# A chunked attention and a SoLU layer: the first eight tiles in a written order, weights converted 1024 columns at a time

## The chip, the cores and the metric

The program runs on one core of a Trainium2 chip. The metric is the device time of one execution in microseconds (us). Five engines run their own instruction streams and wait for each other by semaphores: TensorE (PE in the profile; its weight loads PEld), VectorE (DVE), ScalarE (ACT), GpSimd (POOL) and SyncE (SP), which here only issues transfers.

## The reference

```python
def _attn_ref(q, k, v):                 # 8 batches, 8 heads, 576 positions, 64 wide
    scores = scale * np.matmul(q_c, k_c.transpose(0, 1, 2, 4, 3))   # inside chunks of 64
    scores = scores - np.max(scores, axis=-1, keepdims=True)
    attn = np.exp(scores)
    attn = attn / (np.sum(attn, axis=-1, keepdims=True) + 1e-09)
    out = np.matmul(attn, v_c)

def _moe_ref(x, w_in, w_out, g_ln):     # x: 4608 x 512, from the attention's output
    h = x @ w_in                        # 512 x 1024
    sm = softmax(h)                     # written out with max, exp, sum + 1e-9
    solu = h * sm
    mu, var = mean(solu), mean((solu - mu) ** 2)
    ln = (solu - mu) / np.sqrt(var + 1e-06) * g_ln
    return (ln @ w_out).astype(np.float32)     # 1024 x 512
```

w_in and w_out arrive as 64-bit floats; the kernel reads them as pairs of 32-bit words.

## The kernel before, in words

The 4608 rows are 36 tiles of 128 rows (two chunks of 64). A tile passes these steps: q and k are turned so that their 64 columns lie on partitions (qT, kT); `scores` (16 small products into the PSUM tile sx); `softmax_a` (maximum and difference on VectorE, exponential on ScalarE), `softmax_b` (sum, reciprocal, division); the attention is turned (attn_t); `values` (16 small products, sx again); the result is split into a high and a low part (x_h, x_l); `ffn_in`, 24 products of 512 columns into ph; `solu_a` (maximum h_nmax, exponential) and `solu_b` (the product with h, then the mean); `variance`; z is turned and split (z_h, z_l); `ffn_out` in three thirds of 8 products (po), each started by `third`; `store`. Products with weights use three terms, high by low, high by high and low by high, with the types float32r for both parts. The names are those of the profile.

The weights are converted once from 64-bit words to a high part (wi_h for w_in, wo_h for w_out times g_ln) and a low part (wi_l, wo_l). Before the change this goes in 16 pieces of 512 columns. `piece_scale` takes the absolute value of the upper word, scaled (ScalarE, w_a). `piece_top` clamps it to a range (VectorE or POOL), shifts it left by 3 (VectorE), puts the sign back (VectorE, SCALAR_TENSOR_TENSOR w_a<-w_raw,w_a), masks the exponent (w_p), forms the lower word's part w_r from that (POOL or VectorE), and rounds the high part (ScalarE). `piece_rest` makes the low part: for the ten pieces in `D_PE` by three products on TensorE (the value by the identity or by a diagonal of g_ln, a plain float32 product; minus the high part; w_r) and an evacuation, for three by two such products after a subtraction elsewhere, for three without TensorE.

Tiles 0 to 4 come from a table of words, START, that names the steps in turn (`C:1` converts the next piece, `M:2` is `ffn_in(2)`, `F` a third of an output product). Their order on each engine is set by the library's scheduler from a model of durations, since `order.on` is false there: only from tile 5 on do instructions keep the program's order. From tile 5 a loop runs over the tiles; in an iteration i it does `ffn_in(i)`, the scores of tiles 8, 9 and so on ahead, and the output product of tile i - 3. Tiles 0 to 4 take q and k by natural loads (nat, two halves, one for even and one for odd tiles) and turn them on TensorE (`N`); from tile 5 on they come from loads of a batch in blocks of 32 columns (q_st, k_st), which VectorE turns (`qk_turn`). The raw words w_raw of unit 1 share a buffer with nat's tag z_t, those of units 2 to 7 alternate in the buffers of q_st and k_st, two of each.

Of the kernel before, what the change touches and what calls it, by code (L numbers as in the profile page):

```python
# [8 lines left out]
F32 = mybir.dt.float32  # L9
# [9 lines left out]
P0 n:0 P1 N:0 P:1 n:1 S:0 C:1 P:2 A:0 B:0 P:3 g C:1 n:2 N:1 C:1 C:1 v:0 T:0 C:1 P:4 C:1  # L19
S:1 N:2 C:1 n:3 C:1 C:1 A:1 P:5 P:6 v:1 B:1 V:0 S:2 T:1 M:0 X:0 C:1 A:2 v:2 C:1 P:7 N:3  # L20
B:2 Y:0 C:1 V:1 Q:1 T:2 C:1 n:4 S:3 A:3 v:3 q:8 R:0 V:2 M:1 q:8 X:1 N:4 B:3 S:4 C:1 A:4
q:8 Y:1 M:2 z:0:0 q:8 K:5 X:2 Y:2 T:3 V:3 K:6 C:1 z:0:1 R:1 Q:2 S:5 B:4 T:4 A:5 S:6 v:4
V:4 B:5 T:5 v:5 F F A:6 K:7 C:1 B:6 C:1 R:2 M:3 v:6 Z:2 F z:1:0 X:3 Y:3 S:7 K:8 M:4 q:14 R:3
z:1:1 X:4 A:7 B:7 Y:4 V:5 U:6 F U:7 q:18 Z:3 R:4 v:7 F F
# [3 lines left out]
class Order:  # L28
# [5 lines left out]
    def engine(self, engine):  # L34
        order = self

        class Ordered:
            def __getattr__(self, name):
                make = getattr(engine, name)

                def call(*args, **kwargs):
                    ins = make(*args, **kwargs)  # L42
# [8 lines left out]
def chunk_attention_then_solu_ffn(  # L51
# [90 lines left out]
    pieces = [("in", m, n) for m in range(NCC) for n in range(2)]  # L142
    pieces += [("out", m, 0) for m in range(NFC)]
    def load_pair(x):
# [12 lines left out]
        if x == 0:  # L157
            for n in range(2):
                cols = slice(n * HALF * raw_words, (n + 1) * HALF * raw_words)
                early[n:n] = [(dst[:, cols], src[:, cols])]  # L160
        else:
            nc.sync.dma_start(dst, src)
        for half in range(2):
            raws[pieces[2 * x + half]] = raw[:, half]

    scaled, tops = {}, {}

    def piece_scale(x):

        hi = raws[pieces[x]][:, :, 1]
        y = scaled[x] = work.tile(
            [P, HALF], F32, name="w_a", tag=("w_a", "o_sb")[x % 2]
        )
        act.activation(y, hi.bitcast(F32), AF.Abs, scale=2.0 ** -112)

    def piece_top(x):

        kind, m, n = pieces[x]
        raw = raws.pop(pieces[x])
        lo, hi = raw[:, :, 0], raw[:, :, 1]
        a = scaled.pop(x)
        (pool if x in MIN_POOL else dve).tensor_scalar(
            out=a, in0=a, scalar1=1.875 * 2.0 ** -96, scalar2=0.0, op0=ALU.min, op1=ALU.max
        )
        r = work.tile([P, HALF], F32R, name="w_r")
        if x in R_ACT:  # L190
            act.activation(r, lo, AF.Copy, scale=2.0 ** -52)
        elif x not in R_DVE:
            pool.tensor_scalar(
                out=r, in0=lo, scalar1=2.0 ** -52, scalar2=0.0, op0=ALU.mult, op1=ALU.add
            )
# [21 lines left out]
        if kind == "in":
            cols = slice(n * HALF, (n + 1) * HALF)
            top, d = wi_h[:, m, cols], wi_l[:, m, cols]
            act.copy(top, a)  # L220
            if x not in D_PE:
                (pool if x in D_POOL else dve).tensor_tensor(
                    out=d, in0=a, in1=top.bitcast(F32), op=ALU.subtract
                )
        else:
            top, d, g = wo_h[:, m, :], wo_l[:, m, :], g_sb[:, m:m + 1]
            act.activation(top, a, AF.Copy, scale=g)
            if x not in D_PE:
                dve.scalar_tensor_tensor(
                    out=d, in0=a, scalar=g, in1=top.bitcast(F32),  # L230
                    op0=ALU.mult, op1=ALU.subtract,
                )
        tops[x] = a, top, d, r

    def piece_rest(x):

        kind, m, n = pieces[x]
        a, top, d, r = tops.pop(x)
        if x in LO_TT and x not in D_PE:
            if kind == "in":  # L240
                (pool if x in LO_POOL else dve).tensor_tensor(
                    out=d, in0=d.bitcast(F32), in1=r.bitcast(F32), op=ALU.add
                )
            else:
                dve.scalar_tensor_tensor(
                    out=d, in0=r.bitcast(F32), scalar=g_sb[:, m:m + 1],
                    in1=d.bitcast(F32), op0=ALU.mult, op1=ALU.add,
                )
            return
        if kind == "in":  # L250
            one, one_r = ident, ident_r
        else:
            one_r = small.tile([P, P], F32R, name="g_diag_r", bufs=2)
            one = small.tile([P, P], F32, name="g_diag", bufs=2)
            for t in (one, one_r) if x in D_PE else (one_r,):
                (dve if x in G_DVE else pool).tensor_scalar(
                    out=t, in0=ident, scalar1=g_sb[:, m:m + 1], scalar2=0.0,
                    op0=ALU.mult, op1=ALU.add,
                )
        ps = ps_o.tile([P, HALF], F32, name="po")  # L260
        if x in D_PE:
            pe.matmul(ps, one, a, start=True, stop=False)
            pe.matmul(ps, minus_r, top, start=False, stop=False)
        else:
            pe.matmul(ps, ident_r, d, start=True, stop=False)
        pe.matmul(ps, one_r, r, start=False, stop=True)
        if x in LO_DVE:
# [579 lines left out]
```

## Time and profile before

| | |
|---|---|
| median of 3 runs | 511.1 us (510.99 to 511.14) |
| the profiled execution | 511.61 us, span 509.8 us |
| busy over the span: TensorE, VectorE, ScalarE, POOL | 478.0, 396.1, 265.0, 179.0 us |
| mean granted TensorE clock | 0.983 |
| chain of waits that ended last | TensorE 79%, VectorE 10% |

The profile has a row for each instruction or group: start, duration, engine, line of the kernel, operation, what it writes and reads, count, and in square brackets the idle time before it and what released it. Most instructions come from the helper in line 42 (49 after the change), so names of tiles tell more than lines. A table of stretches gives the busy time of each engine between two moments, with the granted clock of TensorE (1.00 is full), the share of the transfer engines and their rate. In the groups' rows the numbers behind the bar are busy us, mean ns of one, and idle time before. A plain float32 product of 512 columns and a small product show as two rows or a double count each.

### The profile page before, as it was taken

What the parts mean: (1) busy time and instruction counts of PE and PEld (TensorE: products, weight loads), DVE (VectorE), ACT (ScalarE), POOL (GpSimd) and SP (SyncE); (2) the same over time, 40 slices, a digit from 0 to 9 for tenths busy, and PEclk for the clock granted to TensorE, in tenths of its full rate; (3) what the DMA queues carried; (4) which work ended last, traced back from release to release, by engine and by line L of the source; (5) the groups of instructions that cost most, each with busy time, mean ns of one, the idle gap of its engine ahead of it and who ended that gap; (6) DMA issues with size and microseconds to landing.
All of it is one profiled execution on the core that took longest, in us unless ns stands there. A gap on an engine that the chain in (4) does not pass through costs nothing.

```text
span 509.8 us, 11183 instructions
## 1 busy us (share of the span) xinstructions
PE 478.0 (94%) x4190; PEld 385.7 (76%) x4190; DVE 396.1 (78%) x570; ACT 265.0 (52%) x448; POOL 179.0 (35%) x329
## 2 busy tenths in 40 slices
PE   3676969999999999999999999999999999999996
PEld 2354646777888888888888888888888888888875
DVE  5998967797886988797978887879788887854421
ACT  4755963644545545354555546455454453534442
POOL 4583961262514143232415050504151423323300
PEclk9987979999999999999999999999999999999999
DMA  9997799262878677868744859676761716153211
GB/s 278 346 230 138 126 149 133 40 149 59 189 125 200 128 188 155 195 121 181 155 118 111 165 148 160 162 144 176 137 165 47 187 39 186 46 141 97 69 43 41
DMA packets 204454, 72.33 MB, mean 142 GB/s; under 512 B 188592, under 2 KB 189104, under 8 KB 204016
## 3 DMA queue, kind: packets, MB, share of 16 engines
q1 hardware_dynamic: 197552, 58.23, 52.9%
q0 software_dynamic: 6272, 12.60, 9.5%
q8 instruction: 33, 0.54, 0.5%
q10 hardware_dynamic: 576, 0.79, 0.4%
q14 instruction: 21, 0.17, 0.1%
HBM read 36.97 MB, written 9.44 MB: 91 GB/s over the span
## 4 chain that ended last, share of the span: by engine, by line
PE 79%; DVE 10%; SPq 3%; ACT 3%; DMA 2%; issue 2%; POOL 0%; ACTq 0%; DVEq 0%
PE po L42 37%; PE ph L42 35%; DVE w_a L42 4%; PE sx L42 4%; PE tp L42 4%; SPq L42 3%; DMA w_raw<-in_moe_w_in_dram 1%; ACT z L42 1%; DVE h_nmax L42 1%; DVE w_p L42 1%; DVE z L42 1%; DVE s_sum L42 1%; DVE s_e L42 1%; DMA attn_t<-a_b 1%; DMA k_st<-in_k_dram 0%
## 5 line engine op out<-in xcount | busy, mean ns | idle before, releaser
L42 PE MATMUL ph<-wi_l,x_h 128*128 128x512 f32 x288 | 114.6, 398 | 5.5 <-ACT x_h L42 4.8
L42 PE MATMUL ph<-wi_h,x_h 128*128 128x512 f32 x288 | 114.1, 396 | 0.0
L42 PE MATMUL po<-wo_l,z_h 128*128 128x512 f32 (+1 forms) x288 | 113.6, 394 | 0.3 <-ACT z_h L42 0.2
L42 PE MATMUL po<-wo_h,z_l 128*128 128x512 f32 (+1 forms) x288 | 111.7, 388 | 0.0
L42 ACT ACTIVATE z<-ph,h_nmax 128x1024 f32<-128x1024 f32 x36 | 40.2, 1117 | 137.3 <-DVE h_nmax L42 137.3
L42 PE MATMUL po<-wo_h,z_h 128*128 128x512 f32 (+1 forms) x288 | 111.5, 387 | 0.0
L42 POOL TENSOR_TENSOR u<-ssq,eps 128x1 f32<-128x1 f32 x36 | 7.3, 203 | 218.6 <-ACT sq L42 218.6
L42 PE MATMUL ph<-wi_h,x_l 128*128 128x512 f32 x288 | 79.5, 394 | 0.0
L42 POOL DMA_DIRECT2D z_t<-z_b x136 | 67.9, 506 | 17.7 <-DVE z_b L42 12.3
L42 DVE TENSOR_REDUCE h_nmax<-ph 128x1 f32<-128x1024 f32 x36 | 44.0, 1222 | 35.2 <-PE ph L42 35.2
L42 PEld LDWEIGHTS ph<-wi_l,x_h 128*128 128x128 f32 x288 | 55.1, 191 | 19.3 <-ACT x_h L42 6.9
L42 PEld LDWEIGHTS ph<-wi_h,x_h 128*128 128x128 f32 x288 | 55.1, 191 | 11.4
L42 PEld LDWEIGHTS ph<-wi_h,x_l 128*128 128x128 f32 x288 | 54.5, 190 | 11.8 <-DVE x_l L42 0.3
L42 PEld LDWEIGHTS po<-wo_l,z_h 128*128 128x128 f32 x288 | 54.1, 188 | 12.2 <-ACT z_h L42 0.9
L42 PEld LDWEIGHTS po<-wo_h,z_l 128*128 128x128 f32 x288 | 54.1, 188 | 11.5 <-DVE z_l L42 0.4
L42 PEld LDWEIGHTS po<-wo_h,z_h 128*128 128x128 f32 x288 | 54.1, 188 | 10.4
L42 DVE TENSOR_TENSOR z_l<-z_t,z_h 128x1024 fp32r<-128x1024 f32 (+1 forms) x35 | 40.7, 1163 | 20.9 <-ACT z_h L42 20.9
L42 DVE SCALAR_TENSOR_TENSOR z<-ph,z 128x1024 f32<-128x1024 f32 x36 | 44.0, 1221 | 14.5 <-ACT z L42 14.5
L42 ACT ACTIVATE z<-z,z_sum 128x1024 f32<-128x1024 f32 x31 | 35.8, 1154 | 22.1 <-DVE z L42 21.6
L42 DVE STREAM_TRANSPOSE z_b<-z 128x1024 f32<-128x1024 f32 x33 | 39.9, 1208 | 3.2 <-ACT z L42 3.1
L42 ACT ACTIVATE o_sb<-po,r 128x512 f32<-128x512 f32 (+1 forms) x36 | 24.3, 676 | 30.1 <-POOL r L42 21.2
L42 ACT ACTIVATE sq<-z 128x1024 bf16<-128x1024 f32 x36 | 37.6, 1045 | 2.2 <-POOL z L42 2.2
(105 smaller groups left out, 687.9 us busy)
## 6 DMA issues: line engine op xcount, KB each, us to landing
out_dram<-o_sb SPq DMA_DIRECT2D x33, 256.0 KB, 2.5
v_sb<-in_v_dram SPq DMA_DIRECT2D x32, 256.0 KB, 4.2
z_t<-z_b POOLq DMA_DIRECT2D x128, 64.0 KB, 2.6
z_t<-z_b SPq DMA_DIRECT2D x128, 64.0 KB, 2.9
q_st<-in_q_dram SPq DMA_DIRECT2D x112, 72.0 KB, 3.3
k_st<-in_k_dram SPq DMA_DIRECT2D x112, 72.0 KB, 2.9
w_raw<-in_moe_w_out_dram SPq DMA_DIRECT2D x4, 1024.0 KB, 8.6
attn_t<-a_b SPq DMA_DIRECT2D x60, 64.0 KB, 3.7
```

What stands on the lines that cost most here:

```text
L42: ins = make(*args, **kwargs)
```

## The change

- All engines, SP too, keep the order in which the program names the instructions, in the start as well. START is written anew, with steps cut at their hand-overs from one engine to another: each function with a `yield` is entered once for each time that its word stands in the table, and does the next part.
- The conversion goes by 8 units of 1024 columns. POOL (VectorE for unit 4) clamps the upper word with its sign to a symmetric range; ScalarE applies a parametric ReLU whose negative slope is -2^32; VectorE shifts by 3, which brings that factor's exponent bit to the sign's place, so the step for the sign is gone. VectorE masks and forms w_r, always. All 16 halves make their low part by three products on TensorE; ScalarE evacuates 14 of them, VectorE two. POOL builds two diagonals of g_ln for each half of w_out.
- q and k of tiles 5 to 9 are loaded naturally and turned on TensorE; seven of the 20 copies out of PSUM go to VectorE. Batch 1 is not loaded in blocks any more.
- In the start, the softmax's division goes from POOL to VectorE; the mean of tile 3 goes from POOL to ScalarE. The loop is as before except that its first iteration doesn't turn tile 9, and the blocks of a batch are loaded up to those that a turn needs.

```diff
@@ the table START: two lines of each
-P0 n:0 P1 N:0 P:1 n:1 S:0 C:1 P:2 A:0 B:0 P:3 g C:1 n:2 N:1 C:1 C:1 v:0 T:0 C:1 P:4 C:1
-S:1 N:2 C:1 n:3 C:1 C:1 A:1 P:5 P:6 v:1 B:1 V:0 S:2 T:1 M:0 X:0 C:1 A:2 v:2 C:1 P:7 N:3
...
+P0 n:0 v:0 P1 P:1 n:1 P:2 v:1 P:3 N:0:0 N:0:1 N:0:0 n:2 N:0:1 g P:4 S:0 c:0 A:0 c:0 A:0 C:0 B:0
+c:1 t:0 c:1 r:0 T:0 T:0 N:1:0 C:1 N:1:1 D:0:1 N:1:0 t:1 r:1 D:0:0 D:0:1 V:0 N:1:1 D:0:0 c:2
...
@@ the helper through which every engine is called
-                    return order.tc.keep_in_program_order(ins) if order.on else ins
+                    return order.tc.keep_in_program_order(ins)
...
+    EV_DVE = ((1, 0), (5, 1),)
+    NV_DVE = ((0, 0), (0, 1), (1, 0), (1, 1), (3, 0), (6, 0), (9, 1),)
+    MEAN_POOL = (0, 1, 2, 4,)
+    CL_POOL = (0, 1, 2, 3, 5, 6, 7,)
...
+    def unit_scale(x):
+        hi = raws[x][:, :, :, 1]
+        y = scaled[x] = work.tile([P, 2, HALF], F32, name="w_a")
+        top = 1.875 * 2.0 ** 16
+        (pool if x in CL_POOL else dve).tensor_scalar(
+            out=y, in0=hi.bitcast(F32), scalar1=top, scalar2=-top, op0=ALU.min, op1=ALU.max
+        )
+        yield
+        act.activation(y, y, AF.Prelu, scale=2.0 ** -112, alpha=-(2.0 ** 32))
...
+        dve.tensor_scalar(
+            out=au, in0=au, scalar1=3, scalar2=None, op0=ALU.logical_shift_left
+        )
...
+    def unit_high(x):
+        if kind == "in":
+            act.copy(top, a)
+        else:
+            for y in range(2):
+                act.activation(top[:, y], a[:, y], AF.Copy, scale=g)
...
+    def unit_low(x):
+        dve.tensor_scalar(
+            out=ru, in0=au, scalar1=0xFF800000, scalar2=None, op0=ALU.bitwise_and
+        )
+        dve.scalar_tensor_tensor(
+            out=r, in0=lo, scalar=2.0 ** -52, in1=ru.bitcast(F32),
+            op0=ALU.mult, op1=ALU.mult,
+        )
...
+    def unit_rest(x, y):
+        ps = ps_o.tile([P, HALF], F32, name="po")
+        pe.matmul(ps, one, a[:, y], start=True, stop=False)
+        pe.matmul(ps, minus_r, top[:, y], start=False, stop=False)
+        pe.matmul(ps, one_r, r[:, y], start=False, stop=True)
+        yield
+        if (x, y) in EV_DVE:
+            dve.tensor_copy(out=d, in_=ps)
+        else:
+            act.copy(d, ps)
...
-        (dve if order.on else pool).tensor_tensor(
+        dve.tensor_tensor(
             out=e, in0=e, in1=rinv.unsqueeze(2).to_broadcast([P, H, CH]), op=ALU.mult,
...
@@ the word loop
+        if word in begun:
+            next(begun[word], None)
+            continue
+        step = todo[name](*map(int, arg))
+        if step is not None:
+            begun[word] = step
+            next(step, None)
...
@@ the loop from tile 5
             z_turn(i - 1)
-            turn(i + 4)
+            load_batch(next_batch)
+            next_batch += 1
```

VectorE, from its first row of the conversion on. Before, each piece of 512 columns has the clamp and shift (two TENSOR_SCALAR w_a), the sign, the mask w_p and, for some, w_r:

```order
L42 TENSOR_SCALAR w_a<-w_a 128x512 x2
L42 SCALAR_TENSOR_TENSOR w_a<-w_raw,w_a 128x512
L42 TENSOR_SCALAR w_p_154<-w_a 128x512
L42 SCALAR_TENSOR_TENSOR w_r<-w_raw,w_p_154 128x512
L42 TENSOR_SCALAR w_a<-w_a 128x512 x2
L42 SCALAR_TENSOR_TENSOR w_a<-w_raw,w_a 128x512
L42 TENSOR_SCALAR w_p_183<-w_a 128x512
```

```order
L49 COPY qT<-tp 128x512
L49 COPY kT<-tp 128x512
L49 TENSOR_REDUCE s_nmax<-sx 128x8
L49 TENSOR_TENSOR s_e<-sx,s_nmax 128x512
L49 TENSOR_SCALAR w_a<-w_a 128x1024
L49 TENSOR_REDUCE s_sum<-s_e 128x8
L49 TENSOR_SCALAR s_sum<-s_sum 128x8
L49 RECIPROCAL s_rinv<-s_sum 128x8
L49 TENSOR_TENSOR s_e<-s_e,s_rinv 128x512
L49 TENSOR_SCALAR w_p_178<-w_a 128x1024
L49 SCALAR_TENSOR_TENSOR w_r<-w_raw,w_p_178 128x1024
```

The copies and softmax of tile 0 now stand around unit 0, which has one shift, one mask and one product of 1024 columns.

TensorE, from the third quarter of tile 0's input product (ph) on. Before, conversion products of w_out (po with g_diag) wait inside that product:

```order
L42 MATMUL tp<-ident,nat 128x128 x4
L42 MATMUL po<-w_a,g_diag 128x512
L42 MATMUL po<-wo_h,minus_r 128x512
L42 MATMUL ph<-wi_l,x_h 128x512
L42 MATMUL ph<-wi_h,x_h 128x512
L42 MATMUL ph<-wi_h,x_l 128x512
L42 MATMUL po<-w_r,ident_r 128x512
L42 MATMUL sx<-kT,qT 64x64 x16
```

```order
L49 MATMUL tp<-ident,s_e 128x128 x4
L49 MATMUL ph<-wi_l,x_h 128x512
L49 MATMUL ph<-wi_h,x_h 128x512
L49 MATMUL ph<-wi_h,x_l 128x512
L49 MATMUL ph<-wi_l,x_h 128x512
L49 MATMUL ph<-wi_h,x_h 128x512
L49 MATMUL ph<-wi_h,x_l 128x512
L49 MATMUL tp<-ident,nat 128x128 x4
L49 MATMUL sx<-attn_t,v_sb 64x64 x16
L49 MATMUL po<-w_a,g_diag 128x512
```

The products of w_out now stand behind the whole of tile 0's product; those of w_in, which it needs, ahead of it.

SP, from the load of g_ln on (w_raw are the weights, nat the natural q and k):

```order
L679 DMA g_sb<-in_moe_g_ln_dram 128x8x1
L42 DMA v_sb<-in_v_dram 128x8x64
L349 DMA nat<-in_q_dram 128x8x64
L162 DMA w_raw<-in_moe_w_out_dram 128x2x1024 x2
L42 DMA v_sb<-in_v_dram 128x8x64 x2
L349 DMA nat<-in_k_dram 128x8x64
```

```order
L49 DMA g_sb<-in_moe_g_ln_dram 128x8x1
L49 DMA w_raw<-in_moe_w_out_dram 128x2x1024
L49 DMA v_sb<-in_v_dram 64x8x64 x2
L49 DMA nat<-in_q_dram 128x8x64
L49 DMA nat<-in_k_dram 128x8x64
L49 DMA nat<-in_q_dram 64x8x64 x2
L49 DMA nat<-in_k_dram 64x8x64 x2
L49 DMA w_raw<-in_moe_w_out_dram 128x2x1024
```

Units 4 and 5 were loaded next to each other; unit 5 now stands behind the natural loads of tiles 3 and 4.

More of the change, by code (lines that the diff above doesn't have):

```diff
@@ L140, in chunk_attention_then_solu_ffn @@
     raws, early = {}, []
[L142 to L143 removed]
+    UNITS = [("in", m) for m in range(NCC)] + [("out", m) for m in range(NFC // 2)]
     def load_pair(x):
@@ L161, in load_pair, with unit_top @@
         else:
[L162 to L174, printed above, removed]
-        )
[L176 to L184, printed above, removed]
-        a = scaled.pop(x)
[L186 to L195, printed above, removed]
+            sync.dma_start(dst, src)
+        raws[x] = raw
+    scaled, tops, lows, diags = {}, {}, {}, {}
+    def unit_scale(x):
[4 more added lines that the diff above has]
+            out=y, in0=hi.bitcast(F32), scalar1=top, scalar2=-top, op0=ALU.min, op1=ALU.max
+        )
+        yield
+        act.activation(y, y, AF.Prelu, scale=2.0 ** -112, alpha=-(2.0 ** 32))
+    def unit_top(x):
+        kind, m = UNITS[x]
+        if kind == "out" and m == 0:
+            dve.tensor_scalar(
+                out=g_sb, in0=g_sb, scalar1=1.0 / FF, scalar2=None, op0=ALU.mult
+            )
+        lo = raws.pop(x)[:, :, :, 0]
+        a = scaled.pop(x)
         au = a.bitcast(U32)
@@ L217, in piece_top @@
[L217 to L232, printed above, removed]
@@ new lines, in unit_low @@
+            op0=ALU.mult, op1=ALU.mult,
+        )
+        if kind == "out":
+            for y in range(2):
+                one = small.tile([P, P], F32, name="g_diag", bufs=2)
+                one_r = small.tile([P, P], F32R, name="g_diag_r", bufs=2)
+                for t in (one, one_r):
+                    pool.tensor_scalar(
+                        out=t, in0=ident, scalar1=g_sb[:, 2 * m + y:2 * m + y + 1],
+                        scalar2=0.0, op0=ALU.mult, op1=ALU.add,
+                    )
+                diags[x, y] = one, one_r
@@ L250, in piece_rest @@
+        lows[x] = r
+    def unit_rest(x, y):
+        kind, m = UNITS[x]
+        (a, _, top), r = tops[x], lows[x]
         if kind == "in":
             one, one_r = ident, ident_r
+            d = wi_l[:, m, y * HALF:(y + 1) * HALF]
         else:
[L253 to L259, printed above, removed]
@@ L260, in piece_rest @@
-        ps = ps_o.tile([P, HALF], F32, name="po")
[L261 to L267, printed above, removed]
+            one, one_r = diags.pop((x, y))
+            d = wo_l[:, 2 * m + y, :]
+        ps = ps_o.tile([P, HALF], F32, name="po")
+        pe.matmul(ps, one, a[:, y], start=True, stop=False)
@@ L417, in softmax_a @@
         st[i, "e"] = e
-        if not (order.on and i % 2):
-            softmax_e(i)
     def softmax_e(i):
@@ L495, in values, with start_values, start_softmax @@
                     )
-        if not order.on:
-            x_high(i)
-            x_low(i)
+    def start_values(i):
+        values(i)
+        yield
+        x_high(i)
+        yield
+        x_low(i)
+    def start_softmax(i):
+        softmax_a(i)
+        yield
+        softmax_e(i)
     def x_high(i):
```

166 lines of the change are left out of this document (72 added, 94 removed).

## The prediction

> **What bounds the kernel now.** I read the stretches first, cut where the chain of waits changes character.
>
> ```profile
> core 0: us, PE busy (x) PEld busy (x) DVE busy (x) ACT busy (x) POOL busy (x), PEclk, DMA share, GB/s
> 0.00:17.20 17.20, 7.73 (x51) 4.77 (x51) 11.20 (x19) 8.18 (x13) 7.96 (x17) 1.00 0.99 305
> 17.20:46.60 29.40, 18.80 (x119) 11.60 (x117) 28.05 (x44) 17.92 (x34) 17.63 (x17) 0.86 1.00 242
> 46.60:76.40 29.80, 24.78 (x242) 17.66 (x241) 25.09 (x43) 23.57 (x46) 22.99 (x25) 0.85 0.80 127
> 76.40:99.20 22.80, 21.71 (x218) 16.42 (x215) 16.07 (x27) 10.84 (x24) 3.98 (x6) 1.00 0.55 81
> 99.20:127.34 28.14, 27.21 (x297) 22.11 (x298) 23.76 (x37) 14.20 (x26) 12.81 (x22) 1.00 0.46 107
> 127.34:509.80 382.46, 377.80 (x3273) 313.15 (x3271) 291.93 (x405) 190.33 (x307) 113.60 (x244) 1.00 0.60 134
> ```
>
> From 127.34 us on, where the input product of tile 6 starts, TensorE is busy 377.80 of 382.46 us; the change alters next to nothing there, so I carry those 382.46 us over. Before it TensorE has holes, and VectorE is busy 28.05 of 29.40 us between 17 and 47 us. The chain and TensorE's timeline name the point and the holes:
>
> ```profile
> 121.65 5.69 PE po L42 x24
> 127.34 5.44 PE ph L42 x24
> ```
>
> ```profile
> 42.80 2.08 PE L42 MATMUL po<-w_a,g_diag 128*128 128x512 f32 x2 [5.36 <-DVE w_a L42]
> ...
> 49.53 0.40 PE L42 MATMUL ph<-wi_h,x_l 128*128 128x512 f32 x1
> ...
> 70.95 0.79 PE L42 MATMUL ph<-wi_l,x_h 128*128 128x512 f32 x1 [4.37 <-ACT x_h L42]
> 71.54 0.63 PE L42 MATMUL ph<-wi_h,x_h 128*128 128x512 f32 x1
> 71.97 0.63 PE L42 MATMUL ph<-wi_l,x_h 128*128 128x512 f32 x1
> ...
> 76.36 1.19 PE L42 MATMUL ph<-wi_h,x_l 128*128 128x512 f32 x4
> ...
> 80.58 1.02 PE L42 MATMUL po<-w_a,g_diag 128*128 128x512 f32 x2
> 81.44 0.60 PE L42 MATMUL tp<-ident,s_e 128*128 128x128 f32 x4
> 81.80 0.47 PE L42 MATMUL po<-wo_h,z_l 128*128 128x512 f32 x1
> ...
> 84.73 0.69 PE L42 MATMUL sx<-attn_t,v_sb 64*64 64x64 f32 x32
> 85.35 0.66 PE L42 MATMUL tp<-ident,z 128*128 128x128 f32 x4
> ```
>
> The first fence says a tile's 24 products take 5.44 us (0.227 each). The second shows one hole that waits for the conversion's w_a on VectorE (5.36 us), and one of 4.37 us before tile 2's product; after the latter products start 0.43 us apart (71.54 to 71.97), nearly twice the 0.227: a hole is paid twice. From 76.36 us four start within about 1 us again, so half rate held for 5.4 us and cost 2.7 beside the hole's 4.4. Tile 0's product ends at 49.9 us. Prices, start to start: a plain f32 product of 512 columns 0.86 us (80.58 to 81.44), four transposes 0.36, the 16 small products of scores or values 0.62.
>
> The Trainium skill ("TensorE: Matmul & The Clock Gate", Part 1) puts the halving down to an idle window of about 3.4 us, ended by as long a busy one. By that a hole of 4.4 us costs 4.4 + 1.7 us against the rows' 4.4 + 2.7; the rows decide, and I use theirs.
>
> **The change, part by part.**
>
> Conversion on VectorE. Its groups up to 121.6 us:
>
> ```profile
> L42 DVE SCALAR_TENSOR_TENSOR w_a<-w_raw,w_a 128x512 uint32<-128x512 uint32 x16 | 14.7, 924 | 0.2
> L42 DVE TENSOR_SCALAR w_a<-w_a 128x512 uint32<-128x512 uint32 x16 | 10.7, 676 | 0.2
> L42 DVE TENSOR_SCALAR w_p<-w_a 128x512 uint32<-128x512 uint32 x16 | 9.9, 634 | 0.3
> L42 POOL TENSOR_TENSOR s_e<-s_e,s_rinv 128x512 f32<-128x512 f32 x8 | 9.2, 1144 | 16.5 <-DVE s_rinv L42 14.8 <-PE po L42 1.7
> L42 DVE TENSOR_SCALAR w_a<-w_a 128x512 f32<-128x512 f32 x11 | 7.7, 703 | 4.2 <-ACT w_a L42 4.2
> L42 POOL TENSOR_SCALAR z<-z,z_sum 128x1024 f32<-128x1024 f32 x5 | 5.9, 1189 | 9.2 <-DVE z L42 9.0
> L42 DVE STREAM_TRANSPOSE qT<-q_st 128x512 f32<-128x512 f32 x5 | 3.5, 698 | 0.0
> L42 DVE SCALAR_TENSOR_TENSOR w_r<-w_raw,w_p 128x512 fp32r<-128x512 uint32 x4 | 3.5, 868 | 0.3
> L42 DVE SCALAR_TENSOR_TENSOR wo_l<-w_a,g_sb,wo_h 128x512 fp32r<-128x512 f32 x3 | 2.8, 934 | 0.0
> L42 DVE CAST wo_l<-po 128x512 fp32r<-128x512 f32 x2 | 1.4, 688 | 2.3 <-PE po L42 2.3
> L42 ACT CAST z_h<-z_t 128x1024 fp32r<-128x1024 f32 x1 | 1.1, 1052 | 1.0 <-DVE kT L42 1.0
> ```
>
> The VectorE rows of the conversion sum to 14.7 + 10.7 + 9.9 + 7.7 + 3.5 + 2.8 + 1.4 = 50.7 us (smaller ones left out). The sign's SCALAR_TENSOR_TENSOR goes: the Prelu yields the sign. What stays are 8 shifts, 8 masks and 8 products by 1024 columns, one clamp and two evacuations. A shift, mask or product of 1024 columns has no row here. One undisturbed row of 512 bounds it below and two above; I take values near the upper end, because the two masks at 60.05 follow each other without a gap and already hold 1024 columns.
>
> ```profile
> 6.51 0.43 DVE L42 TENSOR_SCALAR w_p<-w_a 128x512 uint32<-128x512 uint32 x1
> 7.06 0.69 DVE L42 SCALAR_TENSOR_TENSOR w_r<-w_raw,w_p 128x512 fp32r<-128x512 uint32 x1
> ...
> 32.11 2.57 DVE L42 TENSOR_SCALAR w_p<-w_a 128x512 uint32<-128x512 uint32 x2
> ...
> 60.05 0.75 DVE L42 TENSOR_SCALAR w_p<-w_a 128x512 uint32<-128x512 uint32 x2
> ```
>
> ```profile
> 7.72 0.69 ACT w_a L42
> ```
>
> So 0.43 to 0.86 for shift and mask (taken 0.8), 0.69 to 1.38 for the product (taken 1.3): 8 x 2.9 + 1.3 + 1.4 = 26 us. VectorE gains 8 softmax divisions from POOL and 7 q/k copies, at the 0.69 of a cast of that width (5.5 and 4.8), and loses ten stream transposes (6.9). Net it drops 50.7 - 26 - 5.5 - 4.8 + 6.9 = 21 us. That is no gain by itself; it ends the waits for w_a.
>
> POOL loses its w_r products, its wi_l and the divisions, and gets 7 clamps of 1024 (bounds: 1.19 from the z row, 2 x 0.87 from 512-wide clamps; taken 1.35) and 16 diagonals. ScalarE's Prelu of 1024 columns lies between 1.05 (z_h) and two of the old passes (0.69 at 7.72); taken 1.1. Eight of these, eight high copies and 14 evacuations replace more than they add, so ScalarE has room: 17.92 of 29.40 us in the table.
>
> TensorE gains work. All 16 halves of the units now take the three products (0.86 + 2 x 0.227 = 1.31 us); before, 10 did and 3 took two. Ten more tile halves of q, k are turned there. Work up to the product of tile 6:
>
> - both: 6 x 24 + 72 products 49.0, 18 score/value groups 11.2, ten transposes of s_e and z 3.6: 63.8 us
> - before: + 10 x 1.31 + 3 x 0.45 + 10 x 0.36 = 81.9 us
> - after: + 16 x 1.31 + 20 x 0.36 = 92.0 us
>
> So 10.1 us are added, and nothing covers them but the holes: 127.34 - 81.9 = 45.4 us of them.
>
> SP. Unit 5's and 6's loads stand behind the natural load of tile 4, which waits for tile 2's turn to free its half of nat. Behind them wait the other q, k and v. By the sum below that turn is over near 28 us; a weight load takes
>
> ```profile
> w_raw<-in_moe_w_out_dram SPq DMA_DIRECT2D x4, 1024.0 KB, 8.6
> w_raw<-in_moe_w_in_dram SPq DMA_DIRECT2D x3, 1024.0 KB, 7.9
> ```
>
> so unit 5 is there near 37 us, ten before TensorE asks for it. The 32 loads of batch 1 (128-byte pieces) disappear, ten natural ones come; they hide, since q, k arrive tiles ahead.
>
> **The sum.** The opening, on one chain. The second half of unit 0 has landed at 7.7 (the row at 7.72 follows its transfer in the chain), and v of tile 0 now goes ahead of it: 256 KB at the 305 GB/s of the first stretch, 0.9 us, so 8.6. Clamp 1.35, Prelu 1.1, shift 0.8, high copy 1.0: 12.9. The division of tile 0 and mask and product on VectorE end near 15.5. TensorE has tile 1's turn ahead of the first unit, and its second bank waits for the attention copies, which stand on ScalarE behind unit 1's Prelu: I get 17.2 us for TensorE's first conversion product, with 2.4 us of work done. From there its order holds 8 x 1.31 + 5.45 (tile 0's product) + 2.4 of small ones = 18.3 us, 35.5 at full clock; it starts cold, so 2 us more: 37.5, where before it was 49.9.
>
> Left are 92.0 - 2.4 - 18.3 = 71.3 us. How dense will they run? Before, 18.7 us of the work were done at 49.9 us (tile 0's product, six conversions, six turns of halves, six small groups), and the other 63.2 took 77.4 us: 82%. From 76.4 us, with the conversion nearly out of the way, TensorE was busy 48.92 of 50.94 us: 96%. In the new order 28 us of TensorE's work stand between tile 0's product and the last conversion, so it reaches to about 69 us; 89%, half of the way between the two, until there and 96% later make 92 to 93%. I take 92. That is 77.5 us: tile 6 starts at 115.0 instead of 127.3, 12.3 us earlier. The profiled execution took 511.61 us (span 509.8), so 499.3; it was 0.5 above the median of 511.1, which gives 498.8: **499 us**. The ends: 100% gives 108.8 (-18.5 us, 492.6); 82% gives 124.5 (-2.8 us, 508.3).
>
> **Rivals.**
>
> *Holes that stay: VectorE behind POOL* (chance 0.18). The two masks at 32.11 took 2.57 us instead of the 0.75 at 60.05, while POOL was at work:
>
> ```profile
> 31.54 1.44 POOL L42 TENSOR_TENSOR s_e<-s_e,s_rinv 128x512 f32<-128x512 f32 x1 [1.74 <-PE po L42]
> 32.94 1.46 POOL L42 TENSOR_TENSOR wi_l<-wi_l,w_r 128x512 fp32r<-128x512 f32 x1
> ```
>
> That is 0.9 us lost for each POOL instruction. The Trainium skill ("SBUF — State Buffer", SBUF: two separate sides) calls it a lock held for a whole instruction; the rows agree. It speaks against making both sides' instructions twice as wide: a blocked shift now waits behind a whole clamp, and all engines follow in a fixed order. The new start has 7 clamps, 16 diagonals and 4 means on POOL. If nine of the 27 hit the chain through the units, 8 us go; or they make one hole as long as that at 70.95, 4.4 + 2.7 us. Either way some 5 us of the 12.3 are left: 506. For it speaks that clamp, shift and mask alternate unit by unit; against it that POOL's two-input work, most of its load (22.99 of 29.80 us in the third stretch), is gone.
>
> *Denser than I think* (0.10). If nothing but the opening is lost, the end is the 492.6 above. Against it: even the stretch from 99.2 us, without conversion, was idle for 0.9 us.
>
> *Slower* (0.07). The conversion's price moves from VectorE to TensorE. If the holes are not VectorE's but come from the order of dependences (weights land, POOL, ScalarE, VectorE, ScalarE, TensorE, ScalarE, each engine in a written order that can't step past a late row), they stay 45.4 us and the 10.1 us of added work come on top: 511.1 + 10.1 = 521. It decides as soon as over 35.3 us are lost. For it: the opening alone loses 17.2 - 2.4 + 2 = 17 us. For it too: the hole at 70.95 is released by ScalarE. Against it: the longest, at 42.80, by VectorE, which was full then.
>
> *No change* (0.03): gains and losses meet within 1 us; nothing pulls there.
>
> **How the numbers follow.** The likeliest case, 92% with 86 to 98% around it, has 0.62 and lies between 494 and 504. With the holes (504 to 509) and the dense case the signs are: faster 0.62 + 0.18 + 0.10 = 0.90, same 0.03, slower 0.07; 0.2% of the time, 1.0 us, is about what a measurement of this kernel tells from no change. The range of 8 in 10 leaves out the slower case, the densest end and the worst of the holes: 493 to 507.
>
> **What would show it.** Right: tile 0's input product ends near 37.5 us (49.9 now), tile 2's starts near 59 (70.95; 19 us of work at 89% lie between), tile 6's near 115, after which the spacing is the old one; VectorE's busy time falls by about 21 us; TensorE's rises by about 10; no hole over 3 us after 20 us. Wrong: a Prelu above 1.4 us or a table load beside it, clamps above 1.8 us, a wait of TensorE for unit 5 or 6, or a clock below 0.9 between 40 and 76 us.

## The result, and the profile after

The changed kernel takes 502.77 us (median of four runs, 502.39 to 504.85) where the kernel before took 511.05 beside it (510.92 to 511.14): a ratio of 0.985, 95% interval 0.982 to 0.987. Forecast were 499.0 and a range of 493 to 507. The profiled execution is the slowest of the four, 504.85 us with a span of 503.1 and a mean granted clock of 0.997; the three others had 1.000 and spans of 500.6 to 501.1.

Stretches of the changed kernel, cut at TensorE's first conversion product, at the end of tile 0's input product, and where the input products of tiles 2, 3, 4 and 6 start:

```profile
core 0: us, PE busy (x) PEld busy (x) DVE busy (x) ACT busy (x) POOL busy (x), PEclk, DMA share, GB/s
0.00:18.83 18.83, 6.20 (x52) 4.84 (x53) 7.84 (x14) 7.48 (x10) 3.56 (x12) 1.00 1.02 301
18.83:39.55 20.72, 20.72 (x133) 13.28 (x132) 16.56 (x23) 13.68 (x22) 5.81 (x6) 1.00 0.92 217
39.55:61.08 21.53, 20.90 (x213) 14.67 (x213) 17.52 (x25) 16.98 (x33) 9.38 (x15) 1.00 0.78 176
61.08:83.80 22.72, 20.99 (x246) 16.27 (x244) 17.68 (x28) 15.96 (x34) 5.78 (x10) 0.99 0.74 137
83.80:96.08 12.28, 11.74 (x111) 9.48 (x110) 7.15 (x11) 5.33 (x10) 0.00 (x0) 0.88 0.38 65
96.08:120.07 23.99, 23.99 (x230) 19.99 (x229) 17.97 (x25) 12.22 (x22) 9.49 (x19) 1.00 0.72 143
120.07:503.10 383.03, 377.92 (x3272) 313.17 (x3271) 291.89 (x405) 190.02 (x307) 113.21 (x244) 1.00 0.59 134
```

The holes are gone: from its first conversion product at 18.83 to the end of tile 0's product at 39.55 TensorE is never idle, and up to tile 6 it is idle for 2.9 of another 80.5 us, 2.8 of them until ScalarE has evacuated a PSUM tile (in total, times, longest):

```profile
PE tp L49 <- ACT attn_t L49: 1.2, 2, 1.0
PE tp L49 <- ACT qT L49: 1.1, 2, 0.8
PE tp L49 <- ACT z_h L49: 0.5, 1, 0.5
```

The last stretch is the old one (382.46 before). The chain of waits places tile 6's product, 127.34 before, here:

```profile
114.38 5.69 PE po L49 x24
120.07 5.44 PE ph L49 x24
```

Now the same span in only two pieces, cut at the end of tile 0's product. First the kernel before, then the changed one:

```profile
0.00:49.93 49.93, 29.86 (x209) 19.07 (x210) 42.14 (x66) 28.32 (x51) 27.63 (x35) 0.90 0.95 250
49.93:127.34 77.41, 70.36 (x711) 53.50 (x711) 62.03 (x101) 46.38 (x91) 37.74 (x51) 0.96 0.62 110
```

```profile
0.00:39.55 39.55, 26.92 (x184) 18.12 (x184) 24.40 (x37) 21.16 (x32) 9.37 (x18) 1.00 0.97 257
39.55:120.07 80.52, 77.62 (x793) 60.40 (x794) 60.31 (x88) 50.49 (x96) 24.65 (x43) 0.98 0.69 138
```

This is the first thing to learn from the result. The opening won 10.4 us, where VectorE's share fell from 42.14 of 49.93 to 24.40 of 39.55. The piece after it *lost* 3.1, because TensorE had 7.3 us more to do there; with 0.6 lost in the last stretch, 6.7 us of span are left. The clock is part of it: with a mean granted clock of 0.983 the kernel before lost (1 - 0.983) x 509.8 = 8.7 us of full TensorE clock, the changed execution at 0.997 some 1.7, and the three at 1.000 none. How much of the 8.7 us fell on products and how much on idle time is not measured.

The groups that carry the new conversion, up to 120 us (busy, mean ns):

```profile
L49 DVE SCALAR_TENSOR_TENSOR w_r<-w_raw,w_p 128x1024 fp32r<-128x1024 uint32 x8 | 10.6, 1331 | 0.3
L49 POOL TENSOR_SCALAR w_a<-w_raw 128x1024 f32<-128x1024 f32 x7 | 8.8, 1253 | 21.6 <-PE po L49 11.8 <-DMA w_raw<-in_moe_w_in_dram 9.2 <-DMA w_raw<-in_moe_w_out_dram 0.6
L49 ACT ACTIVATE w_a<-w_a 128x1024 f32<-128x1024 f32 x8 | 8.5, 1061 | 9.0 <-POOL w_a L49 9.0
L49 DVE TENSOR_SCALAR w_a<-w_a 128x1024 uint32<-128x1024 uint32 x8 | 5.8, 728 | 0.5 <-ACT w_a L49 0.5
L49 DVE TENSOR_SCALAR w_p<-w_a 128x1024 uint32<-128x1024 uint32 x8 | 5.6, 704 | 0.2
```

Product 1.33, clamp 1.25, Prelu 1.06, shift 0.73 and mask 0.70 us: each within 0.1 of what was taken for it (1.3, 1.35, 1.1, 0.8, 0.8). VectorE's busy time over the span fell from 396.1 to 376.6, by 19.5 where 21 were forecast.

### The profile page after: what moved, and what is told of

Read it like the earlier page. It is cut to its first block, busy times and chain, and to the rows that moved or that the text cites. A ratio compares the mean times of both kernels' runs of the same rounds, so it can differ in the third digit from the quotient of the medians.

```text
span 503.1 us, 11184 instructions
## 1 busy us (share of the span) xinstructions
PE 482.5 (96%) x4248; PEld 391.7 (78%) x4248; DVE 376.6 (75%) x529; ACT 261.7 (52%) x434; POOL 147.2 (29%) x305
## 4 chain that ended last, share of the span: by engine, by line
PE 92%; ACT 4%; DVE 1%; issue 1%; DMA 1%; ACTq 0%; SPq 0%
PE po L49 42%; PE ph L49 39%; PE tp L49 7%; PE sx L49 5%; ACT attn_t L49 1%; DMA nat<-in_q_dram 1%; ACT wo_h L49 1%; ACT z_h L49 0%; ACT z L49 0%; ACT o_sb L49 0%; DVE s_e L49 0%; DVE qT L49 0%; DVE h_nmax L49 0%; ACT kT L49 0%; ACT qT L49 0%
## 5 line engine op out<-in xcount | busy, mean ns | idle before, releaser
L49 PE MATMUL ph<-wi_l,x_h 128*128 128x512 f32 x288 | 113.3, 393 | 0.0
L49 PE MATMUL ph<-wi_h,x_h 128*128 128x512 f32 x288 | 112.8, 392 | 0.0
L49 PE MATMUL ph<-wi_h,x_l 128*128 128x512 f32 x288 | 78.0, 389 | 0.0
L49 PEld LDWEIGHTS po<-wo_h,z_l 128*128 128x128 f32 x288 | 54.1, 188 | 11.6 <-DVE z_l L49 0.4
L49 PEld LDWEIGHTS po<-wo_h,z_h 128*128 128x128 f32 x288 | 54.1, 188 | 10.4
L49 ACT ACTIVATE z<-z,z_sum 128x1024 f32<-128x1024 f32 x32 | 36.9, 1154 | 22.2 <-DVE z L49 21.6
```

## The experiments

The question was which part of the change brings the time and which costs it. My theory at the outset was that of the prediction: the lighter conversion ends TensorE's waits for VectorE, the written order keeps TensorE dense, and TensorE is then the bound. The rivals: the conversion alone does it; VectorE is still the pace; wide passes cost hand-over time. Every run stands beside the kernel before on the same chip, whose median there was 511.57 to 511.74. Where two versions are compared below, it is by their distances to the kernel before beside them; for the change that is -8.28 us (502.77 - 511.05).

### The parts, one by one

**Scheduler's order.** All of the change but the order: in the start the engines take the scheduler's order again.

```diff
-                    return order.tc.keep_in_program_order(ins)
+                    return order.tc.keep_in_program_order(ins) if order.on else ins
```

> The changed kernel with one line undone: in the start the scheduler sets the order of the engines again (only from tile 5 on do instructions keep the program's order). If the gain came from the work that left VectorE and POOL, most of it stays: 503 to 506 us. If the written order brought it (TensorE has 20.7 of 20.7 us busy from 18.8 us on in it), the time goes back to 508 to 512 us, with holes of over 2 us on TensorE before 90 us.

Measured: 508.56 us, -3.1, ratio 0.994 (0.991 to 0.997); tile 6 at 123.86. One stretch of it and the wait in it:

```profile
55.00:65.00 10.00, 6.09 (x50) 3.42 (x49) 3.34 (x6) 6.15 (x14) 3.50 (x5) 0.83 1.14 170
```

```profile
58.06 1.12 PE L49 MATMUL po<-w_a,g_diag 128*128 128x512 f32 x2 [2.24 <-POOL g_diag L49]
```

The other parts given, the written order is worth 5.2 us by the medians (8.3 - 3.1). The seven executions spread from 505.75 to 510.76 us, the slower ones at a clock of 0.993. The two at 0.999 or more took 505.75 and 506.30; beside the change's three at 1.000 that leaves about 2.8 us of distance, so part of the 5.2 goes with a lower clock. Between the end of tile 0's product and tile 6, the wait for POOL's diagonal above is the longest of TensorE; a natural load (1.7 us) and an evacuation of z by VectorE (1.4) follow. Copies of q and k end hardly any:

```profile
PE tp L49 <- ACT kT L49: 0.2, 1, 0.2
```

**The recipe alone.** The kernel before with the new steps for a conversion (symmetric clamp, Prelu, shift, mask, product; three products on TensorE for all halves), still in 16 pieces of 512 columns, in the scheduler's order, with the old table and the block loads.

```diff
 (kernel before)
-        act.activation(y, hi.bitcast(F32), AF.Abs, scale=2.0 ** -112)
+        (dve if x // 2 == 4 else pool).tensor_scalar(
+            out=y, in0=hi.bitcast(F32), scalar1=top, scalar2=-top, op0=ALU.min, op1=ALU.max)
+        act.activation(y, y, AF.Prelu, scale=2.0 ** -112, alpha=-(2.0 ** 32))
...
-        dve.scalar_tensor_tensor(out=au, in0=hi, scalar=0x80000000, in1=au, ...
```

> The kernel before with the new conversion alone (clamp, Prelu, shift, mask, product, three products on TensorE for all 16 pieces), in pieces of 512 columns, with its own table of steps, loads in blocks from tile 5 on and the scheduler's order. If the hole before tile 0's product was VectorE's 50 us of conversion, that product ends at 40 to 44 us instead of 49.9 and the kernel takes 504 to 507 us. If only the order counts, TensorE's added 6.8 us of work show and it takes 511 to 518 us.

Measured: 500.60 us, -11.0, ratio 0.978 (0.977 to 0.980): more than the whole change brings. Tile 0's product ends at 36.6 us already, ahead of the 40 to 44 expected. The rest of the change costs 2.8 us net. That was the surprise, and the following runs are about it.

**The recipe in units of 1024 columns.** The run above with the 1024-wide passes of the change, two halves of a unit in the place of two pieces; all else old.

> The recipe alone (before with the new conversion steps, scheduler's order, old table, block loads; 500.6 in pieces of 512), now in units of 1024 columns. Theory W (width costs): most of the 8 us between the two scheduled kernels comes here, 505 to 509, with ph of tile 0 ending some 3 us later (36 to 39) and holes on TensorE before conversion products. Theory N (natural loads cost): 500 to 502, since the passes on VectorE shrink by about 2 us in all.

Measured: 498.52 us, -13.0, ratio 0.974 (0.973 to 0.976): 2.0 us more again. Width does not cost, and this version beats both kernels. That it gains isn't shown: the executions in pieces of 512 had clocks of 0.992 to 0.997, these 0.999 to 1.000, and (1 - 0.993) x 498.7 = 3.5 us of lost clock are more than the 2.0. Its two pieces:

```profile
0.00:40.22 40.22, 29.10 (x221) 18.58 (x222) 23.74 (x34) 24.54 (x39) 12.71 (x24) 1.00 1.01 283
40.22:113.62 73.40, 70.54 (x717) 53.29 (x716) 56.47 (x87) 44.47 (x85) 32.54 (x48) 1.00 0.73 131
```

Tile 0's product ends only 0.7 us later than in the change (40.22 against 39.55), but the second piece is 7.1 us shorter, all of it TensorE's busy time (70.54 against 77.62). Worked out from TensorE's rows (from each start to the next, idle time taken off), the turns of natural q and k have 56 transposes and 6.6 us in the change and 16 and 2.1 here, which is 4.5 us; the conversion products left over by then make 11.6 against 9.4. The remaining difference is 0.6 of slowed input products and small things of both signs.

**Width undone in the change.** Each pass cut in two of 512 columns, same written order.

```diff
-        dve.tensor_scalar(out=au, in0=au, scalar1=3, ...)
+        for n in range(2):
+            dve.tensor_scalar(out=au[:, n], in0=au[:, n], scalar1=3, ...)
```

> The changed kernel with every conversion pass (clamp, Prelu, shift, high copy, mask, product) cut into two of 512 columns that stand next to each other in the same written order; all else as in the change. Both kernels in the scheduler's order differ by 8 us (500.6 with the recipe alone in pieces of 512, 508.6 with all parts of the change but the written order), so either the width or the natural loads to tile 9 cost that much there. Theory W (width costs): a hand-over now needs a pass of half the length: unit 0's chain clamp, Prelu, shift, copy (about 1.3 + 1.06 + 0.73 + 1.0) shrinks by some 2 us, later units' by the same where VectorE waits behind POOL; start of tile 6's product 3 to 5 us earlier, 498 to 500. Theory N (the natural loads cost): the fixed cost of 40 more instructions (some 0.06 us each) on engines that have room; 502 to 504.

Measured: 503.52 us, -8.05, ratio 0.985 (0.983 to 0.987), within 0.3 us of the change. Theory W fell in both orders.

**The recipe with natural loads.** The recipe alone (500.60) with q and k of tiles 5 to 8 loaded naturally and turned on TensorE.

```diff
 (the table: Q:1 and its four q:8 gone, K:5 to K:8 turned into)
+N:5 ... N:6 ... N:7 ... N:8, with n:5 to n:8 each behind the turn that frees its half of nat
```

> The recipe alone (before with the new conversion steps in pieces of 512, scheduler's order), now with q and k of tiles 5 to 8 loaded naturally and turned on TensorE, as the change does, without the block loads of batch 1. Theory N (natural loads cost): 8 halves of four transposes on TensorE (2.9 us and switches), eight copies on ScalarE, and the natural loads wait for the halves of nat and hold SP's queue, the weights behind them: 503 to 508. Theory W (width costs): 499 to 502, the stream transposes gone from VectorE (5.6 us) balance TensorE's work.

Measured: 514.40 us, +2.8, ratio 1.005 (1.004 to 1.007): 13.9 us slower than without, and slower than the kernel before. Up to 50 us the two are alike; then TensorE, between tiles 4 and 5, shows this:

```profile
100.54 0.60 PE L42 MATMUL tp<-ident,nat 128*128 128x128 f32 x4
101.81 0.66 PE L42 MATMUL tp<-ident,nat 128*128 128x128 f32 x4 [0.68 <-ACT qT L42]
103.79 0.66 PE L42 MATMUL tp<-ident,z 128*128 128x128 f32 x4 [1.32 <-ACT kT L42]
...
111.80 0.66 PE L42 MATMUL tp<-ident,z 128*128 128x128 f32 x4 [0.29 <-ACT kT L42]
113.13 0.50 PE L42 MATMUL po<-wo_l,z_h 128*128 128x512 f32 x1 [0.68 <-ACT z_h L42]
```

Turns of q and k, of the attention and of z share the two banks of tp, and the rows show a turn waiting until ScalarE has copied an earlier one out. Two turns in a row make the third wait for a copy; z's turn and the output product behind it come late. The copy of kT that ends the 1.32 us stood on ScalarE behind an exponential of 1.11 us (102.06). Over the piece from tile 0's product to tile 6 TensorE idles 11.4 us (4.8 without the natural loads), the turns themselves cost 4.3 more, and the rest, some 3 us, is spread over the other products; both profiled executions had a clock of 0.993. Of the idle time 4.7 us end with a copy of q or k (1.2 without), so the banks are a part of it and not the whole.

**The same with early natural loads.** Two more buffers (those that batch 1's blocks had), so that tiles 5 to 8 need not wait for a half of nat; the words of their loads stand earlier in the table.

```diff
-                    nat[p0:p1, i % 2, x],
+                    nat_of(i)[p0:p1, i % 2, x],
```

> The recipe alone in pieces of 512 with natural q and k of tiles 5 to 8 (514.4 before this edit, against 500.6 with their block loads), now with two more buffers for them (those that batch 1's blocks had), so that they are loaded from about 35 us on instead of waiting for a half of nat until 55 to 80 us. Theory L (late loads): most of the 13.8 us are waits that follow from loads behind a turn, and TensorE slowed by them; 503 to 506, with only the turns themselves left (8 x 0.45 = 3.6 us). Theory T (the turns and their copies): TensorE and ScalarE have the same work as without this edit, 511 to 514.

Measured: 514.19 us, +2.4, ratio 1.005 (1.003 to 1.007). The loads are issued between 36 and 52 us now, and bring 0.4 us of 13.9. So it isn't that the loads are late; what is left are the turns and their copies, all eight of them on ScalarE. Theory L fell. Which of the two costs more, the turn or ScalarE's copy, no run separates.

**Block loads in the change.** The reverse: in the written order, tiles 5 to 8 by blocks, turned by VectorE.

> The changed kernel with q and k of tiles 5 to 8 loaded in blocks and turned by VectorE as before the change (batch 1 loaded from the table), written order and 1024-wide conversion kept; tile 9 turned on TensorE no longer needed for them. TensorE loses 8 halves of four transposes (0.36 each, 2.9 us, plus switches), VectorE gets 8 stream transposes of 0.70 (5.6) and loses one copy, ScalarE loses seven copies of 0.7. Theory N (the natural loads cost): TensorE's work falls and the time by 2 to 4 us: 499 to 501. Theory W (width costs) with VectorE at the pace, as the run with the sign step put back suggests: the 5 us on VectorE show: 503 to 507.

Measured: 512.05 us, +0.5, ratio 1.001 (1.000 to 1.003), worse than both theories gave. Behind the opening TensorE waits 6.5 us for kT in three waits, one of them long:

```profile
74.24 1.13 PE L50 MATMUL sx<-kT,qT 64*64 64x64 f32 x32 [3.93 <-DVE kT L50]
```

VectorE had run without a gap from 66.97 on and reached this tile's turn at 72.89, right ahead of the scores that need it: my own placing of the turns in its row holds TensorE up there. The clock fell too, to 0.986 in most of the ten executions: (1 - 0.986) x 510.8 = 7.2 us of lost clock, against none in most executions of the change. How the 8.8 us between the two divide into waits and clock is not measured, and the run says little on the loads. A well-placed written order without natural loads wasn't tried.

### Which engine paces the start

**Without the plain float32 products.** 16 products of 0.86 us leave TensorE.

```diff
-        pe.matmul(ps, one, a[:, y], start=True, stop=False)
-        pe.matmul(ps, minus_r, top[:, y], start=False, stop=False)
+        pe.matmul(ps, minus_r, top[:, y], start=True, stop=False)
```

> The changed kernel without the plain float32 product by the identity or the diagonal in the 16 low parts: the low parts of the weights are wrong, 16 x 0.86 = 13.8 us of TensorE's work are gone and nothing else. If TensorE is the bound from 18.8 us on, 9 to 13 us of them come off: 490 to 494 us. If it is full but the chain through ScalarE and VectorE stands right behind, under 5 us come off: 498 to 502 us.

Measured: 498.91 us, -12.7, ratio 0.976 (0.974 to 0.978). Of 13.8 us taken off TensorE 4.5 arrive, as the second theory had it. Three of TensorE's waits up to 130 us:

```profile
PE tp L49 <- ACT attn_t L49: 4.3, 4, 1.6
PE po L49 <- DVE w_r L49: 2.2, 3, 1.4
PE tp L49 <- ACT kT L49: 1.0, 1, 1.0
```

**The sign step back.** Eight SCALAR_TENSOR_TENSOR of 1024 columns more on VectorE, as the old recipe had them.

```diff
+        dve.scalar_tensor_tensor(
+            out=au, in0=hi, scalar=0x80000000, in1=au, op0=ALU.bitwise_and, op1=ALU.bitwise_or)
```

> The changed kernel with the old step for the sign added again, on VectorE: 8 SCALAR_TENSOR_TENSOR of 1024 columns, about 1.25 us each, 10 us in all, with the same result. If VectorE has room now (16.6 of 20.7 and 17.5 of 21.5 us busy), at most 3 us show: 502 to 506 us. If VectorE still sets the pace of the units, 6 to 10 us show: 508 to 513 us.

Measured: 509.70 us, -1.95, ratio 0.996 (0.994 to 0.998). They take 10.8 us on VectorE (1.35 each), and 6.3 of these show, within what the second theory gave.

**The division back on POOL.**

```diff
-        dve.tensor_tensor(out=e, in0=e, in1=rinv...
+        (dve if order.on else pool).tensor_tensor(out=e, in0=e, in1=rinv...
```

> The changed kernel with the softmax's division of the first tiles back on POOL, at the same place of the written order. VectorE loses 8 x 0.69 us (5.5), POOL gets 8 x about 1.14 (9.2) with two inputs. Theory P (VectorE paces, POOL has room): 2 to 5 us faster, 498 to 501. Theory B (POOL's two-input passes hold VectorE off, and clamps and diagonals queue behind them in the written order; the turn of the attention waits 0.5 us longer each time): 503 to 508.

Measured: 508.95 us, -2.8, ratio 0.995 (0.992 to 0.997): 5.5 us slower than the change. TensorE in its opening:

```profile
15.14 1.12 PE L49 MATMUL tp<-ident,s_e 128*128 128x128 f32 x4 [4.82 <-POOL s_e L49]
19.65 1.97 PE L49 MATMUL tp<-ident,nat 128*128 128x128 f32 x8 [3.40 <-ACT attn_t L49]
```

1.18 us per division instead of 0.69, and 1.8 us more on the wait behind it. Theory B's direction held, and the loss went 1 us beyond its range: in the written order, moving the division to VectorE was right, although it loads the busier engine.

**Two low parts on VectorE.** In the fastest version, two of the eight halves of w_out make their low part by two instructions on VectorE instead of three products on TensorE.

```diff
+        if (x, y) in ((5, 1), (7, 1)):
+            dve.scalar_tensor_tensor(out=d, in0=a[:, y], scalar=g, in1=top[:, y]..., op1=ALU.subtract)
+            dve.scalar_tensor_tensor(out=d, in0=r[:, y]..., scalar=g, in1=d..., op1=ALU.add)
+            return
```

> The recipe alone in units of 1024 (498.5), with the low parts of two of the eight halves of w_out (units 5 and 7, second half) made by two SCALAR_TENSOR_TENSOR on VectorE instead of three products on TensorE; four diagonals fall away too. TensorE loses 2 x about 1.2 us, VectorE gets 4 x 0.93 and loses one evacuation. Theory TensorE-bound (TensorE is busy 107 of 110 us between 20 and 130 there): 1.5 to 2.5 us faster, 496 to 497. Theory VectorE paces: 0 to 2 us slower, 498.5 to 500.5.

Measured: 501.80 us, -9.9, ratio 0.981 (0.979 to 0.982): 3.1 us slower than without, beyond both theories. The stretch from 40 to 60 us without the edit, with it, and its longest new wait:

```profile
40.00:60.00 20.00, 18.58 (x163) 12.54 (x163) 16.67 (x23) 17.33 (x33) 13.65 (x19) 1.00 0.84 157
```

```profile
40.00:60.00 20.00, 17.12 (x154) 11.55 (x152) 19.01 (x26) 17.05 (x33) 14.49 (x16) 0.98 0.87 154
57.45 0.33 PE L42 MATMUL sx<-attn_t,v_sb 64*64 64x64 f32 x2 [2.11 <-ACT attn_t L42]
```

VectorE is full there (19.01 of 20 us), and TensorE waits for the attention's copies; that the softmax on VectorE is what makes them late is argued from the stretch. Some of the 3.1 us goes with the clock: the four executions had 0.995 to 0.996 (without the edit 0.999 to 1.000), and (1 - 0.996) x 500.7 = 2.0 us. So two engines pace the start together: load taken off TensorE arrives to a third (4.5 of 13.8), load put on VectorE shows to 58% (6.3 of 10.8).

**One move in the opening.** The first conversion product ahead of tile 1's turn on TensorE.

```diff
-... T:0 T:0 N:1:0 C:1 N:1:1 D:0:1 N:1:0 ...
+... T:0 T:0 C:1 D:0:1 N:1:0 N:1:1 N:1:0 ...
```

> The changed kernel with one move in its table: the first conversion product of unit 0 stands ahead of tile 1's turn on TensorE instead of behind it. The operands are ready at 16.2 (w_r) and TensorE waits 1.59 us for ScalarE's attention copies at that place, so the product would start near 15.5 to 16.2 instead of 18.8. Theory O (the opening's order holds TensorE): tile 0's input product ends 1.5 to 3 us earlier and the time falls by as much: 500 to 501.5. Theory V (VectorE's order holds it: the copies of tile 1's q, k come 2 us later and the following shift and mask behind them): the hole only moves, 502 to 503.5.

Measured: 501.81 us, -9.9, ratio 0.980 (0.979 to 0.982): 1.65 us faster than the change by the distances, 1.0 by the medians as they stand. The first product starts at 15.97:

```profile
15.97 1.92 PE L49 MATMUL po<-w_a,ident 128*128 128x512 f32 x2
...
37.50 0.40 PE L49 MATMUL ph<-wi_h,x_l 128*128 128x512 f32 x1
```

Tile 0's product ends 1.65 us earlier (37.9 against 39.55), and most or all of it is left at the end: theory O, at its lower edge. It is a small gain that the table had left.

## Right and wrong, step by step

- **Faster, since VectorE's drop ends the waits for w_a: right.** The recipe alone, without order and loads, brings 11.0 us, more than the whole change, and 10.8 us of work put back on VectorE cost 6.3 us of the gain. TensorE's waits for w_a up to tile 6's product, in the kernel before and with the recipe alone:

```profile
PE po L42 <- DVE w_a L42: 10.3, 5, 5.4
```

```profile
PE po L42 <- DVE w_a L42: 1.7, 3, 0.9
```

  The changed kernel has none. What the forecast lacked is that the other parts would cost: it gave the turns the price of their transposes alone.
- **The opening: 2.05 us too early.** First conversion product forecast at 17.2, end of tile 0's product at 37.5; they came at 18.83 and 39.55, and so the 20.3 us between the two were right to 0.4. TensorE's row shows what was mis-sized:

```profile
14.37 1.11 PE L49 MATMUL tp<-ident,s_e 128*128 128x128 f32 x4 [4.11 <-DVE s_e L49]
17.07 1.97 PE L49 MATMUL tp<-ident,nat 128*128 128x128 f32 x8 [1.59 <-ACT attn_t L49]
18.83 1.92 PE L49 MATMUL po<-w_a,ident 128*128 128x512 f32 x2
```

  I had named this gate (the turn of tile 1 ahead of the unit, the bank that waits for attention copies), but too early and without the turn behind it: eight transposes from 17.07 on take 1.76 us, twice the 0.87 of eight from 29.93 on, although the table gives that stretch a clock of 1.00.
- **Density: right in kind, and the work beneath it under-priced.** 92% were forecast for what was left; TensorE was busy 77.62 of 80.52 us, 96%. But the 71.3 us of work took 77.6. By kinds, from TensorE's rows: the 8 conversion halves 11.6 us where I had 10.5, the turns of q and k 6.6 for 5.0 (0.47 for four transposes, not 0.36), those of s_e and z 4.0 for 2.9, the output products 17.0 for 16.3, the input products 29.2 for 27.2. Of the latter, 1.3 us are the slowed spell below (tile 3's product takes 6.66 us from its first start to its last, 5.35 in the version with passes of 512 columns). The step that failed is the price list: the 0.36 for four transposes and the 0.86 were each read at one place of the trace, and the mean over the new order is higher. Better density (+4%) paid for half of it; in the total the two errors partly cancel, which is luck.
- **The sum.** Opening +2.05, middle 80.52 - 77.5 = +3.0, the rest 383.03 - 382.46 = +0.6: 5.6, and 499.3 + 5.6 = 504.9, the profiled execution. The median is 2.1 below it; the three executions with a clock of 1.000 took 502.4 to 502.9 us.
- **"Nothing covers the added work but the holes": half right.** With 13.8 us of TensorE's work taken away only 4.5 came, so most of that work *is* covered, by the chain through VectorE and ScalarE that runs just behind.
- **"ScalarE has room", and turns at the price of their transposes: too simple.** The turns of tiles 5 to 9 cost TensorE 4.5 us in the change where ten sets at 0.36 had 3.6, and those of tiles 5 to 8 cost 13.9 us of time with the recipe alone, in the scheduler's order. I priced the transposes and not the wait for a bank, nor the copy's place on ScalarE. That the loads hide, as the prediction says, held: loading early brought 0.4 us. The copies are not what the written order repairs: with all other parts of the change and the scheduler's order only 0.2 us of TensorE's waits end with a copy of q or k.
- **SP: right.** Unit 5 was there at 39.7 us (37 forecast), and no product of TensorE waited for a weight's load.
- **TensorE's busy time: wrong as stated.** It rose by 4.5 us, not 10, since the records before held slowed products (clock 0.90 up to 49.93), which count as busy. With the lost clock of both taken off (8.7 and 1.7 us, at most) the rise is up to 11.5, so the added work itself was priced about right.
- **Rivals.** *VectorE behind POOL* is there, but small:

```profile
26.82 2.02 DVE L49 SCALAR_TENSOR_TENSOR w_r<-w_raw,w_p 128x1024 fp32r<-128x1024 uint32 x1
```

```profile
26.19 1.57 POOL L49 TENSOR_SCALAR w_a<-w_raw 128x1024 f32<-128x1024 f32 x1 [2.30 <-PE po L49]
```

  The product takes 1.22 alone and 2.02 beside the clamp, the clamp 1.11 alone and 1.57 here; after 18.83 TensorE doesn't wait for VectorE once. That is the mechanism of the lock that the prediction cites, at 0.8 us a meeting; one of the eight products met it. With the division on POOL the mean product takes 1.42 us (1.33) and the mean mask 0.78 (0.70). *Slower* needed 35 us of holes; 2.9 were left after the opening. *Denser* is refuted by its own number: at 96% the time still isn't 492.6, since the work was larger.

**What is shown and what isn't.** Shown, along one path and as distances to the kernel before: the recipe -11.0, with the width -13.0; with natural loads to tile 9, division on VectorE and the new table, in the scheduler's order, -3.1; with the written order -8.3. That the natural loads are the harmful one in the third step rests on the run that adds them alone (+13.9, with other places in the table and all copies on ScalarE) and on the 4.5 us of turns in the change; the new table under the scheduler's order was not run by itself. Whether a written order would gain on the fastest version too stays open.

## What to carry to other kernels

Take a change of several parts apart on its best part first: here one part gave more than all, and the written order, which looked like the gain, won 5.2 us back of the 9.9 that the parts before it had cost (13.0 - 3.1). Price a turn on TensorE by its PSUM bank's round trip (transposes, what stands ahead of the copy on its engine, the copy), not by its transposes. Look at the granted clock before you compare two versions: several differences here are no larger than the lost clock. Where two engines stand close behind each other, neither "the bound" nor "room" is a property of an engine: take one instruction's worth of load off each in a run of its own, and believe the shares that arrive.

## What the chip showed unexpectedly

After two short waits of TensorE, 0.75 and 0.98 us, the profiled execution of the change ran tile 3's first products at half rate:

```profile
80.86 0.66 PE L49 MATMUL tp<-ident,s_e 128*128 128x128 f32 x4 [0.75 <-ACT qT L49]
...
83.12 1.03 PE L49 MATMUL tp<-ident,z 128*128 128x128 f32 x4 [0.98 <-ACT attn_t L49]
83.80 0.78 PE L49 MATMUL ph<-wi_l,x_h 128*128 128x512 f32 x1
84.37 0.63 PE L49 MATMUL ph<-wi_h,x_h 128*128 128x512 f32 x1
84.80 0.63 PE L49 MATMUL ph<-wi_l,x_h 128*128 128x512 f32 x1
```

The same place with passes of 512 columns has the same waits, and products 0.23 apart:

```profile
83.07 0.66 PE L49 MATMUL tp<-ident,z 128*128 128x128 f32 x4 [0.98 <-ACT attn_t L49]
...
83.80 0.40 PE L49 MATMUL ph<-wi_h,x_h 128*128 128x512 f32 x1
84.04 0.40 PE L49 MATMUL ph<-wi_l,x_h 128*128 128x512 f32 x1
```

So equal waits are followed by a slowed spell in one execution and not in the other. The granted clock from 83.26 to 86.67 us is 0.50, half of it is 1.7 us, and that is most of what lies between 504.85 and 502.6 us. The Trainium skill ("TensorE: Matmul & The Clock Gate", Part 1) puts the halving down to an idle window of about 3.4 us, and says that the window runs freely, so that the same kernel shows more or fewer slow products from run to run. The second sentence agrees with the four executions of the change, one at 0.997 and three at 1.000. The first isn't settled here: the longest wait here is 0.98 us and the two together are 1.7; but from 78.88 to 83.80 us TensorE ran only transposes, 64x64 products and waits, and whether the clock takes these for idle time no run here shows.

One activation table was loaded in the whole program of the change (1.28 us, at 0.72): Prelu and the exponentials needed no change between them.
